# Two batches of a chunked recurrence in lockstep from chunk 4, and two smaller latency constants in the planner that orders the kernel

## The chip, the cores and the metric

One NeuronCore of a Trainium2 chip runs the whole program. The metric is the time of one execution on the device in microseconds (us); of several runs the median counts.

## What is computed

A recurrence over 768 steps for 4 batches of 8 heads (head size 40), and behind it two layers of a feed-forward network on its output, all in float32.

```python
for t in range(S):
    y[:, :, t] = np.einsum('bhd,bhde->bhe', rt, state)
    Sa = np.einsum('bhde,bhe->bhd', state, at)
    state_decay = state * wt[:, :, None, :] - np.einsum('bhd,bhe->bhde', Sa, bt)
    state = state_decay + np.einsum('bhd,bhe->bhde', vt, kt)
...
x = attn_out.transpose(0, 2, 1, 3).reshape(B * S, H * D)   # 3072 x 320
h = x @ w_in                                               # 320 x 2048
x = (h * tanh(softplus(h))) @ w_out                        # 2048 x 320
h = x @ w2_in
out = (h - tanh(h)) @ w2_out
```

## The kernel before

The 768 steps are cut into 12 chunks of 64 (`NC`, `C`). For every chunk `c` and batch `b` the function `a0` (line 919) makes running products of the decay with scans on VectorE, and `a1` (line 952) multiplies them on TensorE into a triangular matrix `lt` (matmuls `az,wax`) and transposes the keys into `kn` (matmuls `cs,wax`). When all four batches of a chunk have their `lt`, `inv` (line 979) inverts its 16x16 diagonal blocks: two DMAs store `lt` in DRAM (`dm`), one DMA brings the blocks back as `t`, thirty small products on VectorE follow (`t<-t`), and DMAs carry the result back into `X`, by way of `dx`. `merge` (line 1041) then joins the blocks on TensorE (matmuls `t,lt` and `x,t`). This is done two chunks ahead of the recurrence.

The recurrence proper is `steps` (line 1106). For one batch of one chunk it is a chain of stages on TensorE, each with an eviction from PSUM by VectorE or ScalarE behind it that the next stage needs:

- `vu,lt` (16 matmuls), evicted to `z`; `cs,st` transposes the state, evicted to `sn`;
- `x,z` and `z,x` (16 matmuls each), evicted to `vu` and to a half of `rv`;
- `rv` (8 matmuls), masked by VectorE into `lt`;
- `vu,kn` (16), added to the state `st` by VectorE;
- `lt,kn` and `rv,sn` (16 each), evicted to `ah`, and from there to the inputs `xt` and `xs` of layer 1.

Two PSUM banks take turns by the batch's number (`psB`, line 888), one bank is shared by all steps (bank 3), one by `a1` and `merge`. Layer 1 of a chunk (`moe1`, line 1278) runs one chunk later: 16 units, each with eight matmuls into a bank `h` (`unit_in`), and six into `y` (`unit_out`). These are the large matmuls that can fill TensorE while a step's evictions run. The results of layer 1 go to DRAM as `x1d` by way of a tile `isc` that exists once and is also written by the scans of `a0`. `second_pieces` (line 772) converts the weights of layer 2 in small pieces on VectorE (`raw`, `fh`). After chunk 11 layer 2 runs on its own (from 860 us).

What runs when is not the order of the source. Every call is recorded by the class `Plan` as a task with its cost, and `Plan.run` (line 263) sorts the tasks by a list scheduler: `forward` (line 323) puts the ready task with the longest way to the end on its engine, 12 rounds with ranks from `backward` (line 285), and the best round is emitted. All instructions therefore have one line in the profile, 282. Consecutive matmuls are one task until `nc.cut()` is called. A task may start when its predecessors have ended, plus a distance that `add` (line 174) gives to each pair:

```python
lat = 200 if "tensor" in o["alts"] else self.TOPE if engine == "tensor" else 150
```

So `TOPE` (line 99) is the time in ns that the planner leaves between the end of an eviction and the matmul that needs it. For a DMA it books, besides the issue and the packets' time, a landing of `self.LAND + 1000 * far` (line 213; `LAND` is on line 98). The planned times only set the order in each engine's queue: on the chip an instruction starts when its semaphores allow it and everything ahead of it on its engine has started.

`steps` takes a list of batches. With one batch it is the chain above. With two, each stage is written for both before the next begins, without a cut between the two, so that a stage's matmuls of both batches are one task. How many it takes is set on line 1436:

```python
together = 1 if c < PAIR else 2
for b0 in range(0, B, together):
```

`PAIR` is 20, and there are 12 chunks, so it is always one.

Of the kernel before, what the change touches and what calls it, by code (L numbers as in the profile page):

```python
# [31 lines left out]
CUT = 16  # L32
CUTB = 4
SKEW = 2
PAIR = 20
LATER = 2
R2 = 3
LATE = "4444"
# [44 lines left out]
class Plan:  # L83
# [11 lines left out]
    DUTY0 = 4500  # L95
    DRAIN = 95
    NEAR = 600
    LAND = 1500
    TOPE = 300
    SECOND = 3000  # L100

    def __init__(self, nc):
# [71 lines left out]
    def add(self, engine, method, args, kw, *more):  # L174
# [33 lines left out]
        if engine == "sync":  # L208
# [3 lines left out]
            far = ins[0].space == DRAM and (run >= 4096 or run <= 256 and packets > 1000)  # L212
            t["fixed"] = self.LAND + 1000 * far
            if ins[0].space == DRAM and out.name.startswith("raw"):
# [5 lines left out]
        for ap, write in [(a, a.space == PSUM) for a in ins] + [(o, True) for o in outs]:  # L220
            name, p0, p1, lo, hi = self.region(ap)
            ws, rs = self.acc.setdefault(name, ([], []))
            for old, raw in ((ws, True), (rs, False)) if write else ((ws, True),):
                for q0, q1, l, h, o in old:
                    if q0 < p1 and p0 < q1 and l < hi and lo < h and o is not t:
                        if o["alts"].keys() == t["alts"].keys() and len(t["alts"]) == 1:
                            lat = 60 if raw and engine == "vector" else 0
                        else:
                            lat = 200 if "tensor" in o["alts"] else self.TOPE if engine == "tensor" else 150
                        t["preds"][o["id"]] = max(t["preds"].get(o["id"], 0), lat)  # L230
# [386 lines left out]
def fused(ctx, tc, cs, odd, wax0, rv0, wax, rv, vn, cst, w, win1, wout1, win2, wout2, out):  # L617
# [210 lines left out]
    with ExitStack() as p1:  # L828
# [605 lines left out]
        for c in range(NC):  # L1434
            xt = [xp.tile([128, 2, 2, B, C], F32R, tag=n, name=n, bufs=k) for n, k in (("xt", 2), ("xs", 1))]
            together = 1 if c < PAIR else 2
            for b0 in range(0, B, together):
# [243 lines left out]
```

## Time and profile before

| | |
|---|---|
| median of 3 runs | 1221.39 us (1216.62 to 1222.6) |
| the profiled execution, its time | 1215.45 us |
| its span, first to last instruction | 1213.7 us |
| mean granted TensorE clock | 0.974 |
| TensorE busy | 1150.1 us |
| VectorE busy | 900.7 us |
| ScalarE busy | 817.1 us |

The profile calls TensorE PE (its weight loads PEld), VectorE DVE, ScalarE ACT, GpSimd POOL and SyncE SP; SPq is a DMA issue. Names are `output<-inputs` by the program's tiles with buffer numbers left out; every product of the recurrence and of the inverse goes to a tile `ps`. Matmuls are pipelined: the time between two starts is what a matmul costs, and the duration shown for one is longer. A matmul on float32 operands with 128 columns or fewer often stands as two rows in the trace and one in the order below. "issue" as a releaser means that the engine waited for nothing that the profile shows.

### The profile page before, as it was taken

How to read it: one execution, taken by the hardware profiler on the slowest of the kernel's cores; microseconds unless marked ns; L12 is line 12 of the kernel's file. 1: busy time of each engine (PE TensorE's matmuls, PEld its weight loads, DVE VectorE, ACT ScalarE, POOL GpSimd, SP SyncE). 2: the span in 40 equal slices, each digit the busy share in tenths (PEclk: the TensorE clock that was granted, in tenths of full speed). 3: DMA queues.
4: the chain of work that ended last, by engine and by line, in shares of the span. 5: the costliest groups of instructions: out<-in, count | busy, mean ns of one | idle time of the engine just before them, and what ended most of it. 6: DMA issues, size and time to landing. Idle time of an engine off the chain costs nothing.

```text
span 1213.7 us, 38107 instructions
## 1 busy us (share of the span) xinstructions
PE 1150.1 (95%) x15321; PEld 1057.2 (87%) x15321; DVE 900.7 (74%) x2769; ACT 817.1 (67%) x1785; POOL 18.2 (1%) x79
## 2 busy tenths in 40 slices
PE   8989899989999999998899899999999999999996
PEld 7779798988898888888889788899999989999996
DVE  8989798889989897978787977768655444454542
ACT  3544688668787877877677768789685757573322
POOL 1000000000000000000000000000000000000000
PEclk9989899899999999998899999999999999999999
DMA  9456344344434444443434434337855445430001
GB/s 274 131 149 174 92 109 103 88 108 117 99 95 115 105 100 107 94 102 79 113 84 108 101 79 93 75 68 226 254 186 130 144 115 149 132 116 22 11 12 24
DMA packets 255920, 136.09 MB, mean 112 GB/s; under 512 B 190840, under 2 KB 238456, under 8 KB 255736
## 3 DMA queue, kind: packets, MB, share of 16 engines
q1 hardware_dynamic: 255736, 133.58, 43.3%
q8 instruction: 122, 2.00, 0.7%
q14 instruction: 62, 0.51, 0.1%
HBM read 102.06 MB, written 26.61 MB: 106 GB/s over the span
## 4 chain that ended last, share of the span: by engine, by line
PE 49%; DVE 7%; ACT 3%; issue 2%; DMA 1%; SPq 1%; DVEq 0%; ACTq 0%
PE ps L282 25%; PE y L282 12%; PE h L282 12%; DVE t L282 2%; ACT th L282 1%; DVE u L282 1%; DMA x1d<-isc 1%; DMA t<-dm 1%; SPq L282 1%; DVE lt L282 1%; ACT L282 1%; DVE isc L282 1%; DVE gl L282 1%; DVE raw L282 0%; DVE fh L282 0%
## 5 line engine op out<-in xcount | busy, mean ns | idle before, releaser
L282 PE MATMUL y<-wo,gh 128*128 128x320 f32 (+1 forms) x902 | 211.8, 321 | 0.9 <-DVE gh L282 0.6
L282 PE MATMUL h<-xt,wih 128*128 128x256 f32 (+1 forms) x800 | 179.9, 316 | 4.1 <-ACT u L282 2.7
L282 PEld LDWEIGHTS y<-wo,gh 128*128 128x128 f32 x902 | 150.2, 191 | 7.8 <-DVE gh L282 0.7
L282 PE MATMUL y<-wo,gl 128*128 128x320 f32 x448 | 139.7, 312 | 0.4 <-DVE gl L282 0.2
L282 PEld LDWEIGHTS h<-xt,wih 128*128 128x128 f32 x800 | 130.7, 198 | 8.6 <-ACT u L282 3.6
L282 ACT ACT_TABLE_LOAD x98 | 125.7, 1283 | 2.4 <-PEq L1670 0.7
L282 PE MATMUL h<-xt,wil 128*128 128x256 f32 (+1 forms) x400 | 121.5, 304 | 0.1
L282 ACT ACTIVATE th<-th 128x1024 f32<-128x1024 f32 (+2 forms) x107 | 105.7, 988 | 4.2 <-DMA th<-in_wout_dram 2.3
L282 PE MATMUL h<-t,wi 128*128 128x256 f32 (+1 forms) x448 | 102.8, 312 | 0.3 <-DMA t<-xs 0.3
L282 ACT ACTIVATE th<-h,cs 128x256 f32<-128x256 f32 x168 | 77.4, 471 | 33.9 <-PE h L282 32.8
L282 PEld LDWEIGHTS y<-wo,gl 128*128 128x128 f32 x448 | 85.6, 191 | 2.4 <-DVE gl L282 2.2
L282 PEld LDWEIGHTS h<-xt,wil 128*128 128x128 f32 x400 | 79.1, 198 | 2.4 <-issue 0.3
L282 PEld LDWEIGHTS h<-t,wi 128*128 128x128 f32 x448 | 75.2, 197 | 4.6 <-DMA t<-xs 0.5
L282 ACT ACTIVATE rv<-ps 128x128 f32<-128x128 f32 (+1 forms) x133 | 49.0, 384 | 43.8 <-PE ps L282 42.7
L282 DVE TENSOR_TENSOR gl<-u,gh 128x256 fp32r<-128x256 f32 x176 | 72.9, 417 | 7.5 <-ACT gh L282 5.2
L282 DVE TENSOR_TENSOR t<-t 128x15 f32<-128x15 f32 (+4 forms) x360 | 70.8, 197 | 6.6 <-DMA t<-dm 5.0
L282 DVE TENSOR_TENSOR x<-ps,rv 128x512 f32<-128x512 f32 x48 | 33.1, 690 | 56.4 <-ACT rv L282 56.4
L282 DVE TENSOR_TENSOR lt<-ps,cs 128x512 f32<-128x512 f32 x96 | 65.4, 682 | 10.6 <-PE ps L282 10.2
L282 DVE TENSOR_TENSOR x<-h,rv 128x512 f32<-128x512 f32 x48 | 33.1, 690 | 51.3 <-ACT rv L282 51.3
L282 DVE TENSOR_TENSOR u<-th,u 128x256 f32<-128x256 f32 x168 | 66.8, 414 | 5.8 <-ACT th L282 5.6
L282 PE MATMUL h<-zr 128*128 128x256 f32 x496 | 68.7, 293 | 0.0
L282 PEld LDWEIGHTS h<-zr 128*128 128x128 f32 x496 | 63.8, 197 | 1.4
(219 smaller groups left out, 2772.9 us busy)
## 6 DMA issues: line engine op xcount, KB each, us to landing
wax<-in_wax_dram SPq DMA_DIRECT2D x88, 160.8 KB
wax<-in_win_dram SPq DMA_DIRECT2D x20, 512.0 KB
wax<-in_wout_dram SPq DMA_DIRECT2D x20, 512.0 KB
rv<-in_rv_dram SPq DMA_DIRECT2D x92, 64.0 KB
dm<-lt SPq DMA_DIRECT2D x22, 256.0 KB
x<-dx SPq DMA_DIRECT2D x22, 256.0 KB
wo<-w2o SPq DMA_DIRECT2D x8, 640.0 KB
lt<-x1d SPq DMA_DIRECT2D x144, 32.0 KB
```

Of the source, the lines that this page charges most:

```text
L282: getattr(getattr(self.nc, engine), method)(*args, **kw)
```

## The change

Three numbers. `PAIR` goes from 20 to 4: from chunk 4 on `steps` takes two batches at a time, b = 0, 1 and then b = 2, 3, and their stages are planned as joint tasks. `LAND` goes from 1500 to 1200 ns and `TOPE` from 300 to 180 ns: the planner books a shorter landing for each DMA and leaves less between an eviction and the matmul behind it.

```diff
-PAIR = 20
+PAIR = 4
...
-    LAND = 1500
-    TOPE = 300
+    LAND = 1200
+    TOPE = 180
```

No computation is added or taken away: TensorE has 10563 matmuls and transposes in the order before and 10565 after (two more of the fillers that multiply zeros during the setup), SyncE 1169 DMAs in both. The order of nearly every engine differs throughout, since the planner makes it anew.

TensorE, chunk 8 of the recurrence, first batches; `ps_141` and `ps_142` are the banks of an even and an odd batch, `kn_155` and `kn_158` the keys of b = 0 and b = 1. Before, from the end of `vu,kn` of b = 0:

```order
L282 MATMUL ps_141<-vu_120,kn_155 40x40 x8
L282 MATMUL h_148<-xt_168,wih 128x256 x2
L282 MATMUL h_148<-xt_168,wil 128x256
L282 MATMUL h_148<-xt_168,wih 128x256 x2
L282 MATMUL h_148<-xt_168,wil 128x256
L282 MATMUL h_148<-t_151,wi_173 128x256 x2
L282 MATMUL ps_141<-lt_118,kn_155 40x64 x2
L282 MATMUL ps_141<-rv_121,sn_127 40x64 x2
```

Now:

```order
L282 MATMUL ps_141<-vu_120,kn_155 40x40 x8
L282 MATMUL ps_142<-vu_120,kn_158 40x40 x8
L282 MATMUL h_147<-xt_168,wih 128x256 x2
L282 MATMUL h_147<-xt_168,wil 128x256
L282 MATMUL h_147<-xt_168,wih 128x256 x2
L282 MATMUL h_147<-xt_168,wil 128x256
L282 MATMUL h_147<-t_151,wi_173 128x256 x2
L282 MATMUL ps_141<-lt_118,kn_155 40x64 x2
L282 MATMUL ps_141<-rv_121,sn_127 40x64 x2
```

The `vu,kn` matmuls of b = 1 have moved up beside those of b = 0, and one unit of layer 1 follows both; the `lt,kn` and `rv,sn` runs of the two batches stand one behind the other (8 rows each).

VectorE, the inverse of chunk 8, made during the steps of chunk 7: the mask of the chunk's last batch (`lt_118<-ps_143`) starts the round trip, and `t_136<-t_136 128x15` is the first product that needs its end. The last rows ahead of that product. Before:

```order
L282 TENSOR_TENSOR raw_206<-fh_205,raw_206 128x128
L282 TENSOR_TENSOR gl_207<-u_149,gh_169 128x256
L282 TENSOR_TENSOR gl_208<-u_149,gh_170 128x256
L282 STREAM_TRANSPOSE isc_152<-y_146 128x64
L282 STREAM_TRANSPOSE isc_152<-y_145 128x64
L282 STREAM_TRANSPOSE isc_152<-y_145 128x256
L282 TENSOR_TENSOR t_136<-t_136 128x15 x2
L282 TENSOR_TENSOR lt_119<-ps_141,cs 128x512
L282 TENSOR_TENSOR t_136<-t_136 128x28
```

Now:

```order
L282 STREAM_TRANSPOSE isc_152<-y_146 128x64
L282 STREAM_TRANSPOSE isc_152<-y_145 128x64
L282 STREAM_TRANSPOSE isc_152<-y_145 128x256
L282 TENSOR_TENSOR lt_119<-ps_142,cs 128x512
L282 TENSOR_TENSOR lt_119<-ps_141,cs 128x512
L282 TENSOR_SCALAR fh_205<-raw_206 128x128
L282 SCALAR_TENSOR_TENSOR fh_205<-raw_206,fh_205 128x128
L282 TENSOR_SCALAR raw_206<-fh_205 128x128
L282 TENSOR_TENSOR t_136<-t_136 128x15
L282 TENSOR_TENSOR st_129<-ps_141,st_129 128x4x40
L282 TENSOR_TENSOR t_136<-t_136 128x15
L282 TENSOR_TENSOR st_130<-ps_142,st_130 128x4x40
```

The first product now stands 11 rows behind that mask instead of 15 (the mask itself is above the rows shown), and the state adds `st_129` and `st_130` of a pair stand right behind the first two products.

## Rows read from the trace of the kernel before

**Rows 1.** Page, busy us of each engine, share of the span, instructions.
```profile
PE 1150.1 (95%) x15321; PEld 1057.2 (87%) x15321; DVE 900.7 (74%) x2769; ACT 817.1 (67%) x1785; POOL 18.2 (1%) x79
```

**Rows 2.** Busy us by stretch (us, length, PE, PEld, DVE, ACT, POOL, PEclk, DMA, GB/s).
```profile
337.00:822.00 485.00, 455.46 (x8119) 424.26 (x8116) 400.95 (x1383) 373.51 (x838) 8.82 (x38) 0.97 0.42 95
...
860.00:1214.00 354.00, 343.93 (x1919) 311.09 (x1917) 170.24 (x348) 186.77 (x366) 0.00 (x0) 0.99 0.37 102
```

**Rows 3.** TensorE's waits, 337 to 822 us: us in total, times, longest.
```profile
PE ps L282 <- issue: 10.0, 7, 2.2
PE ps L282 <- DVE st L282: 3.2, 5, 1.1
PE ps L282 <- DVE lt L282: 2.7, 3, 1.9
...
PE ps L282 <- DVE sn L282: 0.8, 2, 0.6
...
PE ps L282 <- DVE z L282: 0.7, 2, 0.4
```

**Rows 4.** Timeline, TensorE, chunk 8 (start us, us, instruction, count, [idle before <- releaser]).
```profile
599.25 0.51 PE L282 MATMUL ps<-vu,kn 128*40 128x40 f32 x16 [1.88 <-DVE lt L282]
599.68 0.50 PE L282 MATMUL h<-xt,wih 128*128 128x256 f32 x2
...
602.09 0.44 PE L282 MATMUL ps<-lt,kn 128*40 128x64 f32 x4 [1.06 <-DVE st L282]
...
603.96 0.80 PE L282 MATMUL h<-xt,wih 128*128 128x256 f32 x2
...
605.83 1.82 PE L282 MATMUL ps<-rv 128*128 128x128 f32 x8
```

**Rows 5.** The same timeline, two units of layer 1 behind and ahead of small matmuls.
```profile
607.39 0.50 PE L282 MATMUL h<-xt,wih 128*128 128x256 f32 x2
607.73 0.28 PE L282 MATMUL h<-xt,wil 128*128 128x256 f32 x1
607.85 0.40 PE L282 MATMUL h<-xt,wih 128*128 128x256 f32 x2
...
608.45 0.40 PE L282 MATMUL h<-xt,wih 128*128 128x256 f32 x2
...
609.50 0.67 PE L282 MATMUL ps<-vu,lt 128*64 128x40 f32 x16
```

**Rows 6.** Timeline, VectorE, chunk 8.
```profile
597.12 0.18 DVE L282 TENSOR_TENSOR t<-t 128x15 f32<-128x15 f32 x1 [3.94 <-DMA t<-dm]
...
598.51 0.68 DVE L282 TENSOR_TENSOR lt<-ps,cs 128x512 f32<-128x512 f32 x1
```

**Rows 7.** Busy us by stretch, the stretch at the lower clock.
```profile
600.60:607.40 6.80, 5.74 (x52) 5.28 (x50) 5.46 (x27) 4.67 (x14) 0.00 (x0) 0.50 0.38 108
```

**Rows 8.** VectorE's waits, 140 to 822 us.
```profile
DVE isc L282 <- DMA x1d<-isc: 12.9, 8, 6.1
...
DVE t L282 <- DMA t<-dm: 5.0, 2, 3.9
...
DVE isc L282 <- DMA wax<-in_wax_dram: 4.1, 2, 3.2
```

**Rows 9.** Timeline, SyncE's queue, chunk 8 (time is that of the issue).
```profile
586.50 1.34 SPq L282 DMA_DIRECT2D dm<-lt  x2
```

**Rows 10.** Timeline, VectorE, chunk 5.
```profile
400.76 0.45 DVE L282 STREAM_TRANSPOSE isc<-y 128x256 f32<-128x256 f32 x1 [1.47 <-DMA x1d<-isc]
```

**Rows 11.** Timeline, TensorE, chunk 5.
```profile
401.84 0.66 PE L282 MATMUL ps<-cs,wax 128*128 128x128 f32 x4 [0.53 <-DVE lt L282]
```

**Rows 12.** Page, DMA queues: packets, MB, share of 16 engines.
```profile
q8 instruction: 122, 2.00, 0.7%
```

**Rows 13.** Timeline, TensorE, chunk 7: waits with nothing late.
```profile
557.24 0.26 PE L282 MATMUL ps<-x,z 64*40 64x64 f32 x1 [2.14 <-issue]
...
560.93 0.56 PE L282 MATMUL ps<-x,t 32*16 32x16 f32 x45 [0.77 <-issue]
```

## The prediction

> **What bounds the kernel now.** Read the page's busy shares first: TensorE is busy for 95% of the span, no other engine for more than 87% [rows 1]. Then the same by stage. In the stretch of the joint steps (chunks 4 to 11, 337 to 822 us) TensorE works 455.46 of 485.00 us and VectorE 400.95; in the second layer (from 860 us) TensorE works nearly all the time [rows 2]. So the recurrence is bound by TensorE with VectorE close behind, and the change can only win back what TensorE loses between 337 and 822 us: waits, stretches at the lower clock, and the price of going from one kind of matmul to another. The list of TensorE's waits for that stretch is read next [rows 3]: 10.0 us are put down to "issue" (no semaphore is late), and the largest named ones are the state add `st` (3.2 us) and the masks `lt` (2.7 us), which are both evictions inside a recurrence step. Last comes the timeline of one such place, chunk 8 [rows 4], with VectorE beside it [rows 6].
>
> **Where the joint steps gain: changes of kind.** The order shows all sixteen pairs of chunks 4 to 11 standing together, stage by stage, so the change does what it says. Counted over the whole order, TensorE goes 220 times from small matmuls to large ones and 220 times back; now it is 202 and 202. Changes between two kinds of small matmuls fall from 844 to 816. The price: a unit of layer 1 is eight matmuls of 0.12 us, 0.96 us. The unit that follows small matmuls takes 1.06 us to the next unit's start, and the one that small matmuls follow takes 1.05 us [rows 5]. So entering costs 0.10 us and leaving 0.09 us, and 18 of each are 3.4 us. For the 28 changes among small kinds no row gives a price; it lies between nothing and the 0.10 us of entering, 0 to 2.8 us, and I take the middle, 1.4 us, since they change shape as the others do but reload fewer columns. Term: **-4.8 us** (ends -3.4 and -6.2).
>
> **Evictions covered better.** Each stage ends with an eviction that the next stage waits for. Before, one unit stood between `vu,kn` and `lt,kn` of a batch; now the other batch's `vu,kn` stands there too, 0.43 us more (599.25 to 599.68) [rows 4]. Between `rv` and `vu,kn` stood one large unit and the partner's x,z run; now it is two units beside the partner's `rv`. The joint stage must cover two masks of 0.68 us [rows 6] and does. The waits of step evictions are `st` 3.2, `sn` 0.8 and 0.2 more of a second engine's that I leave alone, and `z` 0.7, together 4.7 us [rows 3]. Of the mask's 1.88 us and the state add's 1.06 us in chunk 8 [rows 4] I count only half, since VectorE itself was late there: its in-order queue had stood 3.94 us behind a DMA, and the mask began at 598.51 us, after it [rows 6]. That is 4.7 - 0.5 + 0.9. Term: **-5.1 us** (ends 0, if the waits only move, and -7.6 with the whole of the mask's and the state add's).
>
> **The clock.** After these two waits the granted clock is 0.50 for 6.80 us [rows 7], the lower of the two levels. There a unit takes 1.87 us (603.96 to 605.83) [rows 4] against 1.06 us at the upper one [rows 5]; so of 5.74 us of work in that stretch 5.74 x (1 - 1.06/1.87) = 2.5 us were lost. Whether the clock still falls with half the wait no row tells: ends 0 and -2.5, I take **-1.2 us**.
>
> **The constants.** TOPE is what the planner allows between the end of an eviction and TensorE's start. Row and row give 0.06 us (the mask ends at 599.19, TensorE starts at 599.25) [rows 4, 6]; 180 ns still lies above that, so I cost it at nothing. Its cover is the 0.12 us that remain; if VectorE runs late by more, it is the first rival's case. LAND is the other way round. Already with 1500 ns VectorE waits for DMAs: 12.9 us for stores to free `isc`, 5.0 us for `dm`, 4.1 us for `wax`, 12 waits [rows 8]. Every landing is now booked 0.3 us earlier, so a consumer that stood at its booked time stands 0.3 us longer: 12 x 0.3 = 3.6 us of VectorE. What TensorE pays for it: for 1.47 us of VectorE 0.53 us later [rows 10, 11], or 0.36 per us; in chunk 8 1.88 + 1.06 for 3.94, or 0.75 per us [rows 4, 6]. I take the 0.36, from a plain store as most of these are: **+1.3 us** (ends 0, as VectorE is idle for a sixth of the stretch, and +2.7). The order of VectorE shows both sides of it: `isc` is rewritten about as soon as before, while the first inverse product now stands much closer behind the mask that its DMA round trip starts from.
>
> SyncE issues the same 1169 DMAs, later or earlier with their stages; none is added, and what stands behind a waiting one is costed with LAND. VectorE loses 13 copies of `u` and 8 of `z` to ScalarE, which is idle for a quarter of the stretch and takes them at no cost unless they meet its table loads; then the wait is among those that I leave as they are. The setup is planned alike (496 filler matmuls before, 497 now), and the second layer is untouched. Chunks 0 to 3 run unpaired and I cost them at nothing.
>
> **The sum**: -4.8 - 5.1 - 1.2 + 1.3 = -9.8 us. Against the profiled execution, 1215.45 us, that is 1205.6 us. The median of the runs, 1221.39 us, lies 5.94 us above the profiled one, so the forecast for a median is **1211.6 us**, 0.8% less. A measurement of this kernel can tell about 0.5% (6.1 us) from no change.
>
> **Rivals.**
> *The waits only move.* The planner drew every queue anew. If each wait that goes comes back at `u`, `kn` or `az`, only the changes of kind and LAND count: -4.8 + 1.3 = -3.5, 1217.9 us, no difference. For it: of the waits on an eviction none has more than five cases in eight chunks [rows 3], so none is a pattern of every chunk. Against: the joined stages have more between them in every chunk.
> *Longer small runs wait for code.* TensorE stands still for 2.14 us at 557.24 and 0.77 us at 560.93 with nothing late, and between those starts lie exactly 128 matmuls [rows 13]: 29 of x,z and z,x, 16 of vu,kn, 83 of x,t. A joint stage puts 64 small matmuls in a row where 32 stood. If that doubles the 10.0 us of "issue" [rows 3], the sum is +0.2, 1221.6 us. Against: most of these waits stand at the merges, which keep their length.
> The Trainium skill, Runtime: NRT & Kernel Launch, section Instruction fetch mechanics, says that code comes in 16 KiB blocks of 256 instructions and that crossing a boundary is mostly hidden. The block size agrees with the queue's 122 packets and 2.00 MB [rows 12], and 256 instructions are 128 matmuls with their weight loads; that the crossing is hidden the 2.14 us contradict. By its rule this rival adds nothing and the 10.0 us would be something else.
> *VectorE stands behind the inverse's round trip (slower).* Each chunk's lt goes to DRAM and comes back as `t` before the inverse's first product. For the inverse of chunk 9, made during the steps of chunk 8, that took 10.62 us, from the store's issue at 586.50 [rows 9] to 597.12 [rows 6]. In the new order the first product of the inverse of chunk 8 stands 11 rows behind the mask, where 15 stood; for chunk 6 it is 15 for 30, for chunk 7 16 for 22; and the state add of the pair is queued directly behind it. If the trip outlasts what TensorE has between the `az,wax` that feeds the mask and that `lt,kn` (an estimate from adding durations over the order: 11 to 12 us), the pair's state adds come late. One such case cost TensorE 1.88 + 1.06 us [rows 4] and the 2.5 us of clock, 5.4 us; in three chunks 16.3 us. Sum +6.5, 1227.9 us: slower. It decides once the trip takes about 1 us longer than the 10.62 us.
> *More waits go than the evictions'.* If joint stages spare another 10 us of the named waits, 1201.6 us.
>
> **How the numbers follow.** Forecast 0.43, more waits go 0.10, waits only move 0.19, code 0.09, round trip 0.19. Faster: 0.43 + 0.10 = 0.53. Within 0.5%: 0.28. Slower: 0.19. The forecast's own ends (-6.2 - 7.6 - 2.5 + 0 = -16.3 and -3.4 + 2.7 = -0.7) give 1205 to 1221 us. To leave out no more than 2 in 10 the range goes down to the last rival, 1201 us, and up past the round trip, 1230 us.
>
> **What would show it.** Right: TensorE's `st`, `sn` and `z` waits in the joint chunks fall from 4.7 to about 1 us; its busy time stays within a few us of 1150; VectorE's waits for `x1d`, `dm` and `wax` rise from 22 to some 26 us; "issue" stays near 10 us. Wrong: `st` waits that stand, VectorE waiting several us for `dm` at those three inverses, or "issue" near 20 us. If the span falls or rises by more than 20 us, the price lies in a stage that I costed at nothing: chunks 0 to 3 or the setup.

## The result and the profile after

| | before | after |
|---|---|---|
| median of 4 runs each | 1219.01 us (1213.11 to 1222.6) | 1201.2 us (1197.28 to 1202.51) |
| ratio, 95% interval | | 0.9876 (0.9832 to 0.9919) |
| the profiled execution, its span | 1215.45, 1213.7 us | 1200.37, 1198.6 us |
| mean granted clock | 0.974 | 0.981 |

The ratio is taken over the fast executions of both kernels; the two medians alone give 0.985. The change makes the kernel 1.2% faster, 0.8 to 1.7 with the interval; 0.8% was forecast. The median lies just inside the lower end of the range (1201 to 1230 us).

The page's busy shares of the changed kernel, to hold against [rows 1]:

```profile
PE 1136.4 (95%) x15323; PEld 1048.4 (87%) x15323; DVE 896.7 (75%) x2774; ACT 811.1 (68%) x1781; POOL 18.2 (2%) x78
```

TensorE was to stay near 1150 us and lose waits instead. It is busy 13.7 us less, with the same matmuls. So the time came out of the busy part. Where, the stretch view tells: the joint chunks (now 333 to 805 us) and the second layer, to hold against [rows 2] (us, length, PE, PEld, DVE, ACT, POOL, PEclk, DMA, GB/s):

```profile
333.00:805.00 472.00, 442.39 (x8043) 417.33 (x8042) 392.43 (x1367) 376.72 (x848) 8.16 (x36) 0.98 0.43 97
...
845.00:1199.00 354.00, 342.94 (x1912) 309.82 (x1911) 175.59 (x369) 181.76 (x362) 0.00 (x0) 0.99 0.38 104
```

The stretch is 13.0 us shorter and TensorE works 13.1 us less in it (455.46 before). What is left, length less busy, is 29.5 us before and 29.6 now: the total of the waits has not moved. Their list for the same stretch, to hold against [rows 3]:

```profile
PE ps L282 <- issue: 11.9, 8, 2.8
PE h L282 <- ACT u L282: 4.3, 6, 1.3
PE ps L282 <- DVE x L282: 2.4, 3, 1.1
PE ps L282 <- DVE lt L282: 2.0, 6, 0.5
...
PE h L282 <- issue: 1.1, 1, 1.1
...
PE ps L282 <- ACT sn L282: 0.5, 1, 0.5
...
PE ps L282 <- DVE z L282: 0.3, 1, 0.3
PE ps L282 <- DVE st L282: 0.3, 1, 0.3
```

The state add, `sn` and `z` are down from 4.7 to 1.1 us, as forecast; but `u`, `x` and "issue" hold more than before. There, besides the 10.0 us of "issue" in [rows 3], stood:

```profile
PE h L282 <- ACT u L282: 2.4, 3, 1.4
...
PE ps L282 <- DVE x L282: 0.5, 1, 0.5
```

Which matmuls the busy time came from stands in TensorE's groups by form (count | busy us, mean ns of one | idle before). First the kernel before, 337 to 822 us:

```profile
L282 PE MATMUL ps<-rv 128*128 128x128 f32 x256 | 35.7, 284 | 0.0
...
L282 PE MATMUL ps<-z,x 64*64 64x40 f32 x512 | 27.6, 222 | 0.0
L282 PE MATMUL ps<-x,z 64*40 64x64 f32 x512 | 25.3, 230 | 3.2 <-issue 2.1 <-DVE sn L282 0.8 <-ACT sn L282 0.2
...
L282 PE MATMUL ps<-vu,kn 128*40 128x40 f32 x448 | 14.0, 212 | 2.1 <-DVE lt L282 1.9
```

and the changed kernel, 333 to 805 us:

```profile
L282 PE MATMUL ps<-rv 128*128 128x128 f32 x256 | 31.1, 275 | 0.0
...
L282 PE MATMUL ps<-z,x 64*64 64x40 f32 x512 | 24.0, 219 | 0.0
L282 PE MATMUL ps<-x,z 64*40 64x64 f32 x512 | 22.7, 226 | 0.5 <-ACT sn L282 0.5
...
L282 PE MATMUL ps<-vu,kn 128*40 128x40 f32 x448 | 12.0, 212 | 1.6 <-issue 1.1 <-DVE lt L282 0.5
```

The four groups, same counts, are busy 4.6 + 3.6 + 2.6 + 2.0 = 12.8 us less (some 1 us of it at the lower clock; other groups went down and up). They are stages of the recurrence that now run as one piece of two batches. What one piece saves is plain in the timeline. Before, one batch's `vu,kn` lasts 0.43 us to the next start (599.25 to 599.68, [rows 4]) and one batch's `vu,lt` 0.59 us when a unit follows:

```profile
618.52 0.67 PE L282 MATMUL ps<-vu,lt 128*64 128x40 f32 x16
619.11 0.56 PE L282 MATMUL y<-wo,gh 128*128 128x320 f32 x2
```

Now both batches together last 0.74 us (590.92 to 591.66) and 1.06 us (645.01 to 646.07):

```profile
590.92 0.81 PE L282 MATMUL ps<-vu,kn 128*40 128x40 f32 x32
591.66 0.50 PE L282 MATMUL h<-xt,wih 128*128 128x256 f32 x2
...
645.01 1.13 PE L282 MATMUL ps<-vu,lt 128*64 128x40 f32 x32
646.07 0.57 PE L282 MATMUL y<-wo,gh 128*128 128x320 f32 x2
```

That is 2 x 0.43 - 0.74 = 0.12 and 2 x 0.59 - 1.06 = 0.12 us for each pair that became one piece. In the traces, matmul by matmul, the time goes at the end of a run: from the last `vu,kn` to a unit's first matmul it is 0.14 us from start to start, between two `vu,kn` 0.02 us in the mean. One run has one last matmul.

VectorE's waits for DMAs (140 to 822 us), to hold against [rows 8], have not grown in all (19.6 us, 23.3 before), though those for `x1d` have, and none is for `dm`:

```profile
DVE isc L282 <- DMA x1d<-isc: 15.4, 12, 4.2
...
DVE fh L282 <- DMA raw<-in_wout_dram: 3.5, 2, 2.3
...
DVE t L282 <- DMA x<-dx: 0.7, 1, 0.7
```

### The profile page after: what moved, and what is told of

It reads as the page before. It is cut to its first block, busy times and chain, and to the rows that moved or that the text cites. A ratio compares the mean times of both kernels' runs of the same rounds, so it can differ in the third digit from the quotient of the medians.

```text
span 1198.6 us, 38122 instructions
## 1 busy us (share of the span) xinstructions
PE 1136.4 (95%) x15323; PEld 1048.4 (87%) x15323; DVE 896.7 (75%) x2774; ACT 811.1 (68%) x1781; POOL 18.2 (2%) x78
## 4 chain that ended last, share of the span: by engine, by line
PE 61%; DVE 16%; ACT 9%; DMA 7%; issue 4%; SPq 1%; DVEq 0%; ACTq 0%
PE ps L282 29%; PE h L282 17%; PE y L282 15%; ACT th L282 3%; DMA x1d<-isc 2%; DVE t L282 2%; DVE u L282 2%; DVE lt L282 2%; DMA wax<-in_w_dram 1%; SPq L282 1%; ACT L282 1%; DVE x L282 1%; DVE isc L282 1%; DVE gl L282 1%; DVE raw L282 1%
## 5 line engine op out<-in xcount | busy, mean ns | idle before, releaser
L282 PE MATMUL h<-xt,wih 128*128 128x256 f32 (+1 forms) x800 | 175.6, 310 | 5.0 <-ACT u L282 4.7
L282 ACT ACTIVATE th<-th 128x1024 f32<-128x1024 f32 (+1 forms) x107 | 105.5, 987 | 2.0 <-DVE t L282 0.2
L282 DVE TENSOR_TENSOR lt<-ps,cs 128x512 f32<-128x512 f32 x96 | 64.4, 682 | 14.3 <-PE ps L282 12.8
L282 DVE TENSOR_TENSOR x<-ps,rv 128x512 f32<-128x512 f32 x48 | 33.1, 690 | 51.3 <-ACT rv L282 51.3
```

The source lines that it names most:

```text
L282: getattr(getattr(self.nc, engine), method)(*args, **kw)
```

## The experiments

Every kernel below was timed in five rounds beside the kernel before; that kernel's median was 1214.31, 1214.18 and 1213.31 us beside the three batches. The batches are e1, e2, e5, e6; then e8 to e11; then e12, e13, e7.

**Which part of the change does it.** The pairing alone, the constants alone, and each of the two kernels with its constants nudged, so that the planner draws its queues anew.

```diff
# e1, against the kernel before
-PAIR = 20
+PAIR = 4
# e2, against the kernel before
-    LAND = 1500
-    TOPE = 300
+    LAND = 1200
+    TOPE = 180
# e5, against the kernel before
-    LAND = 1500
-    TOPE = 300
+    LAND = 1490
+    TOPE = 295
# e6, against the changed kernel
-    LAND = 1200
-    TOPE = 180
+    LAND = 1210
+    TOPE = 185
```

> Joint steps alone, both constants as before. Theory A (the joint stages cover their evictions and change kind less often): most of the 1.2% is here, ratio 0.988 to 0.993, and TensorE's waits for st, sn and z between 337 and 822 us fall from 4.7 us to about 1 us. Theory B (the constants do it): ratio 0.998 to 1.002. Theory C (any new order of the queues moves the time by about 1% either way, whatever made it new): no relation to the parts; this one anywhere from 0.985 to 1.01.

> LAND 1200 and TOPE 180 alone, one batch at a time. Theory A: little, 0.998 to 1.004, VectorE waiting somewhat longer for stores (22 to some 26 us between 140 and 822 us). Theory B: ratio near 0.988. Theory C: anywhere from 0.985 to 1.01, and the product of this ratio with that of the joint steps alone need not be near 0.988.

> The kernel before with both constants moved by a trifle (LAND 1490, TOPE 295), which changes no mechanism and only makes the planner draw its queues anew. Theories A and B: within 0.3% of the kernel before. Theory C: off by 0.5% or more.

> The changed kernel with both constants moved by a trifle (LAND 1210, TOPE 185): a new draw of the same mechanisms. Theories A and B: ratio to the kernel before within 0.3% of 0.988. Theory C: off from that by 0.5% or more.

Ratios measured: e1 0.9867 (0.9816 to 0.9918), e2 1.0062 (1.0027 to 1.0097), e5 1.0041 (1.0012 to 1.0069), e6 0.9867 (0.9823 to 0.9911). The lockstep is the whole gain, and theory B is out. The constants add nothing to it, and alone they cost about as much as a nudge of 10 and 5 ns does. The nudge moved the kernel before by 0.4%, between the bounds of theories A (0.3%) and C (0.5%), and the changed kernel by 0.1%. So a new draw alone can be worth some 0.4% here, and whether the constants cost something of their own stays open. Two expectations of theory A missed: the waits for `st`, `sn` and `z` in the stretch of chunks 4 to 11 are 2.6 us in e1, not about 1, and VectorE's waits for `x1d`, `dm` and `wax` in e2 are 21.2 us, not 26.

**Is it the price of a change of kind?** e10 puts one dummy matmul of 16 columns between the two batches of a joint stage, with another number of rows than its neighbours; e11 puts the same with the same number of rows. One of the four places, in e10 (e11 has `0:128` for `0:64` here; at `x,z` it is 128 rows in e10 and 64 in e11):

```diff
+                if i:
+                    nc.tensor.matmul(pbs[i][0:64, 200:216], lts[i][0:64, 0, 0, :], vus[i][0:64, 0, 0, 0:16], start=True, stop=True)
                 for h in range(NP):
                     for g in range(2):
                         p0, q0 = 64 * g, 64 - 64 * g
```

> The changed kernel with 47 dummy matmuls, one between the two batches of every joint stage of four kinds (state by lt, x by z, state by kn, masked by kn), 16 columns each, into columns of PSUM that nobody reads; the computation is not changed. Here each dummy has another number of rows than its neighbours (64 among matmuls of 128, 128 among matmuls of 64). Theory D: 94 more changes between kinds, at 0.13 us each about +12 us against the kernel of e11 (ends: 47 x 0.13 = 6 and 94 x 0.16 = 15). Theory E (changes of kind cost nothing by themselves): the same as e11 within 0.3%.

> The control of e10: the same 47 dummy matmuls in the same places, with the same number of rows as their neighbours, so that no change of kind is added; the computation is not changed. Every theory: 47 matmuls at 0.02 to 0.04 us are 1 to 2 us more than the changed kernel, ratio 0.988 (0.984 to 0.993).

The count in these expectations is wrong: 8 chunks, two pairs and four stages, less the last chunk's `vu,kn`, are 62 dummies and 124 changes, so theory D meant 16 us (8 to 20) and e11 some 2 us. Measured: e10 1.0001 (0.9971 to 1.0031), e11 0.9901 (0.9863 to 0.9939). The difference is 0.0100 x 1214 = 12 us, 0.2 us for each dummy and 0.1 for each change; by the intervals 6 to 18 us. Theory E (changes of kind cost nothing) is out: 62 dummies with their neighbours' rows cost 3 to 4 us (0.9901 against 0.9876 of the changed kernel and 0.9867 of e6, in other batches), with other rows the whole gain. The planner orders e10 and e11 anew too, so a part of their difference in time may be the draw; the rows decide. The row of each in the stretch of chunks 4 to 11, e10 first, then e11:

```profile
341.10:826.80 485.70, 459.41 (x8157) 431.10 (x8156) 397.98 (x1365) 375.71 (x847) 9.45 (x36) 0.98 0.41 94
```

```profile
332.90:805.50 472.60, 445.75 (x8162) 421.14 (x8160) 399.73 (x1385) 368.66 (x828) 9.31 (x36) 0.98 0.42 96
```

13.7 us of busy time lie between them, with equal waits (26.3 and 26.8 us) and an equal clock. (e10's profiled execution, 1221.42 us, is 6 us above its median.) A joint `vu,kn` with its dummy in the timeline of TensorE, e10 and then e11:

```profile
544.77 1.11 PE L282 MATMUL ps<-vu,kn 128*40 128x40 f32 x34
545.82 0.50 PE L282 MATMUL h<-xt,wih 128*128 128x256 f32 x2
```

```profile
489.71 0.89 PE L282 MATMUL ps<-vu,kn 128*40 128x40 f32 x34 [0.22 <-DVE lt L282]
490.53 0.56 PE L282 MATMUL y<-wo,gh 128*128 128x320 f32 x2
```

1.05 us against 0.82, so 0.23 us for two changes: the 0.12 us a piece that the pairs showed. 62 times 0.23 us are 14.3 us, for the 13.7 measured.

**Batches parted, and lockstep from other chunks.** e9 keeps the code stage by stage, but puts a cut between the two batches:

```diff
             for i in turn:
+                nc.cut()
                 for h in range(NP):
```

in all six joint stages on TensorE. e8, e12, e13 and e7 are the changed kernel with another `PAIR`: 1, 2, 6 and 8.

```diff
-PAIR = 4
+PAIR = 1
```

> The changed kernel with its code still written stage by stage for both batches, but with a cut between the two batches in every stage on TensorE, so that the schedule may put other work between them and may let one batch run ahead of the other. In the written order the changes between kinds rise from 1273 to 1339 (before: 1362). Theory D (changes between kinds): 26 more between small kinds and 40 more to or from large ones, 26 x 0.13 + 40 x 0.1 = about 7 us more than the changed kernel, ratio to the kernel before about 0.993, running time outside waits in chunks 4 to 11 back to about 440 us (before 444.6, changed 435.0), and 80 or more of the 110 changes between small kinds are there again. Theory E (the stage by stage order of the evictions and of the stages itself gives the time, whatever lies between the batches): ratio stays at 0.987.

> The changed kernel with the steps of both batches in lockstep from chunk 1 on (was: from chunk 4 on). Theory D: the gain is that TensorE changes less often between kinds of matmuls (each change costs about 0.13 us at the start of the next kind), not that it waits less. In the written order the changes fall from 1273 to 1233, of which 30 are between two small kinds: 30 x 0.13 + 10 x 0.1 = about 5 us less than the changed kernel, some 1194 to 1197 us, ratio to the kernel before 0.983 (0.978 to 0.988). Theory W (the gain comes from waits that later chunks have, where the recurrence is behind): chunks 1 to 3 give nothing, ratio as the changed kernel's, 0.987, or worse, because the start of the kernel has other work that is due.

> The changed kernel with lockstep from chunk 2 on (was: from chunk 4 on). In the written order the changes between kinds fall from 1273 to 1246, 23 of them between two small kinds. Theory D (the number of changes alone sets the time): 23 x 0.13 + 4 x 0.1 = about 3 us less than the changed kernel, ratio to the kernel before 0.984 (0.980 to 0.988). Theory F (changes set the running time, but every new schedule draws its waits and its half-clock stretches anew, and lockstep in the early chunks draws badly, as e8 did from chunk 1 on): running time at full clock outside waits falls all the same, but waits and half clock rise, and the ratio lies between the changed kernel's 0.987 and e8's 1.001.

> The changed kernel with lockstep from chunk 6 on. Changes between kinds in the written order 1301 (changed 1273, before 1362): 18 more between small kinds and 10 more to or from large ones, 18 x 0.13 + 10 x 0.1 = 3.3 us more than the changed kernel. Theory D: ratio to the kernel before 0.990 (0.986 to 0.994). Theory F: the same 3.3 us of running time, and a draw of waits and half clock of up to 0.5% either way on top: 0.985 to 0.997.

> The changed kernel with lockstep from chunk 8 on, so in 4 chunks in place of 8. Changes between kinds in the written order 1335: 26 more between small kinds and 36 more to or from large ones than in the changed kernel, 26 x 0.13 + 36 x 0.1 = 7 us more. Theory D: ratio to the kernel before 0.993 (0.989 to 0.997). Theory F: the same, and up to 0.5% either way on top: 0.988 to 1.000. A theory in which the late chunks alone give the whole gain: 0.987.

Measured: e9 1.0033 (1.0004 to 1.0063), e8 1.0008 (0.9981 to 1.0035), e12 0.9896 (0.9859 to 0.9934), e13 0.9972 (0.9943 to 1.0002), e7 0.9999 (0.997 to 1.0027). By the time alone theory D misses all five, always towards slower (e12 only by its median: the interval reaches into 0.980 to 0.988). e9's theory E (0.987) and the theory that the late chunks alone give the gain (0.987 for e7) are out as well. Theory W allows e8's time, but not its reason: the gain does not come from waits, as the table shows. So the time of one stretch was taken apart, for the profiled execution of each kernel: from the moment when TensorE had done 240 of its 1073 us of work to that of 690 (chunks 4 to 11; work counts every matmul at its mean distance to the next start at the upper clock, the same for all kernels). Waits are length less busy, by the stretch view. "Lower clock" is what the matmuls that started at the lower level took beyond that mean, worked out matmul by matmul from the trace; "running" is busy less that. "Changes" are those in TensorE's whole order as the expectations count them, with `x,z` and `z,x` taken as one kind, and `lt,kn` and `rv,sn` as another; some 730 of them are among the large matmuls of both layers and much the same in every kernel (1362 - 440 - 196 = 726 before, 1273 - 404 - 140 = 729 now).

| kernel | lockstep from | changes | length | running | waits | lower clock |
|---|---|---|---|---|---|---|
| before | never | 1362 | 483.7 | 444.7 | 29.5 | 9.5 |
| e5 | never | 1395 | 487.7 | 446.4 | 33.1 | 8.2 |
| e2 | never | 1379 | 496.2 | 448.1 | 34.5 | 13.6 |
| e7 | 8 | 1335 | 489.9 | 442.9 | 37.0 | 10.0 |
| e9 | 4, parted | 1339 | 493.0 | 438.9 | 32.4 | 21.7 |
| e13 | 6 | 1301 | 478.5 | 437.4 | 30.8 | 10.4 |
| after | 4 | 1273 | 471.5 | 435.0 | 29.6 | 6.9 |
| e1 | 4 | 1278 | 471.9 | 435.2 | 29.8 | 6.9 |
| e6 | 4 | 1272 | 480.1 | 433.7 | 33.4 | 13.0 |
| e12 | 2 | 1246 | 467.8 | 437.1 | 29.7 | 1.0 |
| e8 | 1 | 1233 | 493.2 | 436.7 | 42.5 | 14.1 |

The running column follows the count of changes to within some 4 us: 445 to 448 us without lockstep, 434 to 437 with it from chunk 6 or earlier, 438.9 and 442.9 for e9 and e7 between. What e12 and e8 spare beyond chunk 4 lies ahead of this stretch, where by the same split they run for 299.8 and 299.9 us and the other kernels of the table for 300.8 to 307.6. e9's forecast of "about 440" holds; its time doesn't, since 21.7 us went to the lower clock.

The last two columns together go from 31 to 57 us, a spread larger than the gain, and follow no count. It is not the planner's draw alone, for a table of single executions holds their chance too. Beside e8 to e11 the kernel before, one and the same order, took from 1206.04 us at a mean granted clock of 0.978 to 1221.94 us at 0.965, and the profiled executions of e7, e9 and e12 lie 6.9 and 6.4 us above and 5.8 us below the medians of their kernels. A part does belong to the order: the median of the mean clock over all executions is 0.9755 in e8 and 0.9725 in e9, and 0.980 to 0.984 in the changed kernel, e1, e6, e11 and e12. The kernel before has 0.973 to 0.9745, so some of the measured gain is the clock too; e5 and e2, with 0.9815 and 0.980, are slower all the same. Theory F fits e12, e13 (by its interval) and e7; it was made after e8, and its ranges are wide.

In e8, whose stretch begins at 325.5 us, 7.7 before the changed kernel's (mostly since the lower clock took nothing there and 7.6 us in the changed kernel), the loss is plain in TensorE's waits in this stretch:

```profile
PE ps L282 <- issue: 14.8, 10, 2.8
PE h L282 <- ACT u L282: 6.5, 6, 1.9
PE ps L282 <- DVE lt L282: 4.3, 8, 1.0
PE ps L282 <- DVE t L282: 3.1, 6, 1.0
PE ps L282 <- DVE ah L282: 2.8, 3, 1.9
PE ps L282 <- ACT az L282: 2.3, 1, 2.3
```

and in its rows at the seam of chunks 3 and 4, where the clock is at the lower level for 10.2 us from 341.4:

```profile
340.22 1.13 PE L282 MATMUL ps<-vu,lt 128*64 128x40 f32 x32 [1.88 <-DVE ah L282]
341.60 0.80 PE L282 MATMUL h<-xt,wih 128*128 128x256 f32 x2 [0.24 <-ACT u L282]
...
345.93 1.44 PE L282 MATMUL ps<-az,wax 128*128 128x128 f32 x5 [2.25 <-ACT az L282]
```

Whether starting the lockstep early makes these waits, or the planner's draw does, was not tried; it stays open. No version beats both kernels: e12 is level with the changed one (0.9896 and 0.9876, the intervals overlap), though its profiled execution, the quickest of its runs, has a span of 1192.0 us.

## Why the prediction was right, and where it was not

The side was right and the mechanism was among the terms; two terms were mis-sized, in opposite directions. That the sum came near is luck: -4.8 and -5.1 were forecast for the changes of kind and the waits, and about -10 and 0 were measured. The sign "busy time stays within a few us of 1150" failed.

- **Changes of kind, -4.8 us forecast, -9.7 measured** (running 444.7 to 435.0). The step that failed is "changes between two kinds of small matmuls fall from 844 to 816". The count went by names, so it held the alternations of `x,z` with `z,x` and of `lt,kn` with `rv,sn`. These change no shape that costs anything (they start about 0.03 us apart), and longer joint stages hold more of them, 676 for 648. Without them the fall is 196 to 140: 56, not 28. And the price, 0 to 0.10 with 0.05 taken, is 0.12 us by the joined pairs and by e10. 56 x 0.12 = 6.7 us; with the 3.4 us taken for the large changes that is 10.1, for 9.7 measured. That the sum meets so well is in part chance. The 0.10 and 0.09 us of [rows 5] lie in the units' own time, while the 0.12 us lie at the end of the small run ahead of a unit, so such a change costs both. And 11 of the 56 lie among matmuls between which a change is free (last section). Counted in the traces of the stretch alone, runs of one kind fall from 413 to 341 (with `rv`, `az,wax`, `cs,wax` and `cs,st` as one kind and either half of layer 1 as one), 0.13 us each.
- **Evictions covered better, -5.1 forecast, 0.1 the other way measured.** `st`, `sn` and `z` went as forecast, and so did the mask's long wait: the longest `lt` wait is 0.5 us, where it was 1.9 (in e1 it is 2.0). But `u` took 4.3 us for 2.4, `x` 2.4 for 0.5, and "issue" 13.0 for 10.0. For this term the first rival, "the waits only move", was right. Its time, 1217.9 us, was not, since it kept the small price of the changes. The move is no chance of one draw: `st`, `sn` and `z` take 1.1, 2.6 and 1.0 us in the stretch of the changed kernel, e1 and e6, and 4.9, 9.4 and 11.6 (ScalarE's `sn` included) in the kernel before, e5 and e2, while units of layer 1 wait for ScalarE's `u` for 4.3, 7.8 and 7.4 us with lockstep and 2.4, 0.2 and 1.8 without. Why `u` comes later was not tried. The term's lower end, -7.6, counted the state add's 1.06 us twice and should be -6.6; the range did not hang on it.
- **The clock, -1.2 forecast.** The stretch gave 2.6 us (9.5 to 6.9). Against e6 (13.0) and e1 (6.9) that is part of the draw, as is most of the 4.5 us by which chunks 0 to 3 were quicker (337.7 to 333.2; 336.5 in e1, 327.6 in e6), costed at nothing.
- **LAND, +1.3 forecast.** VectorE's waits for `x1d`, `dm` and `wax` were to rise from 22 to some 26 us; waits for DMAs of all kinds are 19.6. They go with the draw and not with LAND: 23.3, 29.1 and 18.0 us with 1500 (before, e5 with its 1490, e1), 19.6, 27.9 and 23.9 with 1200 (changed, e6 with its 1210, e2). e1 and e6 differ in both constants and have one ratio, 0.9867. With lockstep the term is nothing that can be measured.
- **Code.** "issue" is 13.0 us in the stretch, for 10.0. In e1 and e6, with the same joint stages, it is 7.3 and 7.6; in e5 and e2, without them, 8.2 and 7.9. So the longer small runs don't raise it, and the rival falls. The stalls themselves stay: the longest in the changed kernel is 3.1 us (200.1 us), and in the stretch three pairs of them stand 127 matmuls of the trace apart, such as those before 616.9 and 620.8 us. By the Trainium skill, Runtime: NRT & Kernel Launch, section Instruction fetch mechanics, crossing a block of code is mostly hidden. The trace agrees, other than the prediction had it: 8043 matmuls in the stretch are some 63 blocks, with the prediction's 128 matmuls to a block, and 9 such waits stand there. Those nine cost the 13.0 us.
- **The round trip.** VectorE does not wait for `dm` in the changed kernel. The order put the inverse's first product nearer to the mask, and the trip was over in time (one store is issued at 520.36 us, and the first product runs at 528.39 without a wait). In e2, without lockstep, VectorE waits for `dm` for 6.9 us, TensorE 10.2 us for `st` in the stretch, and the kernel is 0.6% slower: rival and mechanism go together there, but that one causes the other is not shown. Against it, TensorE waits 7.3 us for `st` in e5, where VectorE never waits for `dm`, and only 1.4 us in e1, where it does for 4.3 us.

By stretches the profiled gain of 15.1 us is 9.7 (running) + 2.6 (lower clock) - 0.1 (waits) in chunks 4 to 11, 4.5 before them, less 1.2 us lost after (378.2 to 379.4) and 0.4 us at the ends.

## What to carry to other kernels

Where an engine is busy for 95% of the time, look into the busy time before the waits: count the places where one shape of matmul follows another, by rows and tile rather than by name, and read a price from one run standing alone against two in one, on both sides of the change. When a planner draws every queue anew, make a second draw of both kernels by a nudge before a difference of half a per cent is believed, and don't read the lower clock's share from one execution. A chain that is made shorter can hand its gain to the next wait, so check the sum of the waits and not the one that was meant.

## What the runs showed of the hardware that was not expected

- A run of small matmuls costs 0.12 us at its end when another shape follows. In e10 and e11 the number of rows alone differs: a 16-column dummy of 64 rows among matmuls of 128 costs 0.23 us more than one of 128 rows. Not every change has the price. `lt,kn` and `rv,sn`, both 128 rows by 40 columns, alternate in groups of four every 0.11 us. From `vu,kn` (128 by 40) to `vu,lt` (128 by 64) it is 0.03 us from start to start (26 cases in the 13 traces, at the upper clock), and between `x,z` and `z,x` (64 by 40, 64 by 64) 0.02. But from small matmuls of 128 rows to the 128 by 128 ones it is 0.15 us (197 cases), and from 64 rows to small ones of 128 also 0.15 (44 cases).
- The lower clock took between 1.0 and 21.7 us in kernels that compute the same with nearly the same waits (e12 and e9: 29.7 and 32.4 us in the stretch). The order of the queues is one part of it and the chance of the single execution another; what decides it in these schedules the runs don't show.
